# Attention in blocks of 64 tokens on 64x64 tiles of the array, with parts of the next product between its steps

## The chip, the core and the metric

The kernel runs on one core of a Trainium2 chip. The time is in device microseconds (us), and the kernel before has a median of 674.34 us over two runs (673.64 and 675.03). Engines: TensorE (PE, its weight loads apart as PEld), VectorE (DVE), ScalarE (ACT), GpSimd (POOL), and SyncE (SP), whose queue issues nearly all DMA transfers.

## The reference, cut to what matters

Inputs: q, k, v of shape (4, 8, 768, 64), fp32; one decay lam per head; then U (768, 32), V (32, 768), w_ch1 (512, 2048) and w_ch2 (2048, 512), which arrive as 64-bit numbers.

```
for b in range(12):                       # blocks of 64 tokens
    intra = (qb @ kb.T * Dmask) @ vb      # Dmask[i, j] = lam ** (i - j) for i >= j, else 0
    inter = (qb * lam ** (pos + 1)) @ kv_state
    out[block] = intra + inter
    kv_state = lam ** 64 * kv_state + (kb * lam ** (63 - pos)).T @ vb
x = out, as (4, 768, 512)                 # heads side by side
u = x + (x.T @ U @ V).T                   # mixing over the 768 tokens, rank 32
result = u + relu(u @ w_ch1) @ w_ch2
```

## The kernel before

The kernel has three stages.

**The front** walks through NS = 24 steps: 4 sequences of NT = 6 tiles of P = 128 tokens each, all 8 heads in a step (HP = 4 pairs of heads, two to the 128 rows of the array). Although the reference uses blocks of 64 tokens, a step treats its 128 tokens as one block, with a decay mask of 128 by 128 and one state update for the step. The work is cut into named pieces, and the list `pieces` is an order written out by hand: in this stage every engine runs its instructions in just this order. A step s has on PE: `prep` (transposes of q and k of step s + 1, L348, which ACT copies out as qt and kt, L351), `scores` (pss, L393), `inter` (q times the held state, px, L434), `intra` (masked scores times v, px, L446) and `state` (pkv, L411). DVE multiplies the scores by the mask (sm, L402) and adds up the state (kv, L419); POOL scales k (ks, L365) and the transposed q (qs, L376); ACT fades the old state (L385) and copies the result out (x_nat, L451). An fp32 matmul is two instructions in the profile.

Six to seven steps later a finished tile goes on: once a sequence has its six tiles, `low` (L461) makes x.T @ U, DVE and ACT split it into parts (`low_rows`, `next_of_low`), and `mix` (L506) multiplies by V; DVE adds that to x (L509). `turn` transposes u (L523), writes u to memory (u_d, issued on SP) and splits it into a high part, a low part and a difference (u_hl, u_d; L528, L539, L542, L543). Meanwhile `aside` converts the 64-bit weights into three such parts on DVE and ACT (L154 to L217); w1 tiles 0 and 1 are made in the front.

**The first product** takes w1 tile by tile (FT = 16) against u in NG = 6 groups of 512 tokens: `hidden` takes two groups at a time and makes for each 8 matmuls into pz (L722) and 4 into pd (L732). ACT takes pz out into a tile r (L728), DVE adds pd (L737), and SP writes r to memory. The first eight calls (`head`) also carry the last tiles' mix and turn, put between their matmuls by the lists `rest` and `at`.

**The second product** reads r back, applies the relu and splits it (L837 to L840), and multiplies with w2 (L855, L857, L859) into all eight PSUM banks, four pairs per group. `finish` takes each pair out through a tile o: ACT (L876), DVE (L880), POOL (L884), a write issued on SP (L885). The tiles r and o share one pool:

```
r_pool = ctx.enter_context(tc.tile_pool(name="r", bufs=4, reuse_waits="tile"))
...
o = r_pool.tile([P, C], FP32, tag="r", name="o")
```

From the end of `head` on, the order of instructions comes from the framework's planner and not from a list. A tile from a pool with n buffers waits until the tile n before it under the same tag has been read for the last time.

## Time and profile before

| | before |
|---|---|
| median of the runs | 674.34 us (673.64 to 675.03) |
| profiled execution, span from first to last instruction | 672.5 us |
| lowest and highest run less that span | 1.1 and 2.5 us |
| PE, PEld busy | 665.9 us (99%), 545.4 us (81%) |
| DVE, ACT, POOL busy | 496.6 (74%), 278.7 (41%), 112.8 us (17%) |
| front ends (first pz matmul starts) | 121.45 us |
| granted TensorE clock, mean | 0.999 of full |

The profiled execution has no time of its own beside its span; the runs lie 1.1 to 2.5 us above it. In the profile, a line like `28.78 1.16 PE L393 MATMUL ... x16` is a merged group: start and length in us, engine, line of the kernel, shape and count. A group's length includes the drain of its last matmul, so that the cost of a group in a stream of work is the distance from its start to the next group's start. PE counts as busy while any matmul is under way; that it is busy doesn't mean that it is at its peak.

### The profile page before, as it was taken

To read this page: it belongs to the slowest core of one execution; us is meant where nothing else is said; L and a number is where in the kernel's file an instruction comes from. 1 tells how busy PE (TensorE), PEld (TensorE's weight loads), DVE (VectorE), ACT (ScalarE), POOL (GpSimd) and SP (SyncE) were. 2 spreads that over 40 slices of the span, in tenths; PEclk is the share of its full clock that TensorE was granted. 3 is DMA by queue.
4 is the path that set the end of the run, shared out by engine and by line. 5 is a ranking of instruction groups with operands and counts; after the bars stand their busy time and mean duration, and the time that the engine had idled before them with its cause. 6 is when DMAs were issued, how large, how long until landed. Compare 5 with 4: busy or idle time off the path is not lost.

```text
span 672.5 us, 13170 instructions
## 1 busy us (share of the span) xinstructions
PE 665.9 (99%) x5124; PEld 545.4 (81%) x5124; DVE 496.6 (74%) x873; ACT 278.7 (41%) x517; POOL 112.8 (17%) x92
## 2 busy tenths in 40 slices
PE   9999999999999999999999999999999999999997
PEld 8888898787888888888888888888888888888885
DVE  4679999777999777777797255786586775865854
ACT  4675767454555444444455121332232322322320
POOL 4455667340000000000000000030030200300300
PEclk9999999999999999999999999999999999999999
DMA  9999993264776555555587999854363363443421
GB/s 208 214 228 239 237 232 109 84 215 156 235 276 240 204 203 204 204 203 204 203 280 253 325 314 387 291 185 140 94 206 107 110 204 94 158 155 95 161 89 62
DMA packets 131775, 131.27 MB, mean 195 GB/s; under 512 B 81346, under 2 KB 89794, under 8 KB 131714
## 3 DMA queue, kind: packets, MB, share of 16 engines
q1 hardware_dynamic: 130656, 130.18, 61.3%
q8 instruction: 40, 0.66, 0.4%
q10 hardware_dynamic: 1058, 0.26, 0.2%
q14 instruction: 21, 0.17, 0.1%
HBM read 80.09 MB, written 50.33 MB: 194 GB/s over the span
## 4 chain that ended last, share of the span: by engine, by line
PE 96%; DVE 2%; ACT 2%; issue 0%; DVEq 0%; ACTq 0%
PE pz L722 27%; PE pz L857 13%; PE pd L732 13%; PE pz L855 13%; PE pd L859 13%; PE pss L393 3%; PE px L446 3%; PE put L523 2%; PE pq L348 2%; PE px L434 1%; PE pkv L411 1%; PE pk L348 1%; PE pp L461 1%; PE pu L506 1%; PE idle L336 0%; ACT qt L351 0%
## 5 line engine op out<-in xcount | busy, mean ns | idle before, releaser
L722 PE MATMUL pz<-u_hl,w 128*128 128x512 f32 x768 | 190.4, 397 | 0.0
L722 PEld LDWEIGHTS pz<-u_hl,w 128*128 128x128 f32 x768 | 144.0, 188 | 35.5 <-issue 0.4
L857 PE MATMUL pz<-w_hl,m 128*128 128x512 f32 x384 | 151.1, 396 | 0.0
L855 PE MATMUL pz<-w_hl,m 128*128 128x512 f32 x384 | 150.9, 396 | 0.0
L859 PE MATMUL pd<-w_d,m 128*128 128x512 f32 x384 | 149.5, 396 | 0.0
L838 ACT ACTIVATE m<-mt 128x512 fp32r<-128x512 f32 x96 | 60.7, 633 | 196.0 <-PE pd L859 141.7
L839 DVE SCALAR_TENSOR_TENSOR m<-rm,m 128x512 fp32r<-128x512 f32 x96 | 71.4, 745 | 52.2 <-ACT m L838 52.1
L884 POOL TENSOR_TENSOR o<-o,u 128x512 f32<-128x512 f32 x20 | 29.9, 1529 | 447.3 <-DVE o L880 447.3
L737 DVE SCALAR_TENSOR_TENSOR r<-pd,r 128x512 f32<-128x512 f32 x96 | 61.8, 685 | 54.0 <-ACT r L728 43.5
L732 PE MATMUL pd<-u_d,w 128*128 128x512 f32 x384 | 98.6, 397 | 0.0
L728 ACT ACTIVATE r<-pz 128x512 f32<-128x512 f32 x96 | 52.2, 596 | 93.6 <-PE pz L722 92.9
L857 PEld LDWEIGHTS pz<-w_hl,m 128*128 128x128 f32 x384 | 72.3, 188 | 17.7
L855 PEld LDWEIGHTS pz<-w_hl,m 128*128 128x128 f32 x384 | 72.3, 188 | 17.6
L859 PEld LDWEIGHTS pd<-w_d,m 128*128 128x128 f32 x384 | 72.3, 188 | 17.6
L732 PEld LDWEIGHTS pd<-u_d,w 128*128 128x128 f32 x384 | 72.1, 188 | 17.3
L840 DVE SCALAR_TENSOR_TENSOR m<-m 128x512 fp32r<-128x512 f32 x96 | 69.0, 720 | 0.9
L837 DVE TENSOR_SCALAR mt<-rm 128x512 uint32<-128x512 uint32 x96 | 46.1, 481 | 28.0 <-DMA rm<-r_d 27.6
L402 DVE TENSOR_TENSOR sm<-pss,mask 128x512 f32<-128x512 f32 x48 | 30.8, 683 | 7.4 <-PE pss L393 7.3
L205 ACT CAST w<-wt 128x512 fp32r<-128x512 f32 x32 | 19.9, 622 | 30.5 <-DVE wt L202 23.4
L376 POOL TENSOR_TENSOR qs<-qt,powq 128x512 f32<-128x512 f32 x20 | 25.9, 1296 | 23.3 <-ACT qt L351 22.3
L446 PEld LDWEIGHTS px<-vraw,sm 128*64 128x64 f32 x768 | 24.7, 137 | 6.0 <-issue 2.4
L446 PE MATMUL px<-vraw,sm 128*64 128x64 f32 x768 | 28.3, 226 | 0.5 <-DVE sm L402 0.4
(88 smaller groups left out, 682.7 us busy)
## 6 DMA issues: line engine op xcount, KB each, us to landing
r_d<-r SPq DMA_DIRECT2D x96, 256.0 KB, 2.5
rm<-r_d SPq DMA_DIRECT2D x96, 256.0 KB, 2.7
words<-in_moe_w_ch_dram SPq DMA_DIRECT2D x30, 512.0 KB, 4.4
w_d<-w SPq DMA_DIRECT2D x16, 768.0 KB, 3.3
w_hl<-w_d SPq DMA_DIRECT2D x16, 512.0 KB, 6.2
vraw<-in_v_dram SPq DMA_DIRECT2D x24, 256.0 KB, 4.6
u_d<-x_nat SPq DMA_DIRECT2D x24, 256.0 KB, 3.5
u<-u_d SPq DMA_DIRECT2D x24, 256.0 KB, 4.1
```

Of the source, the lines that this page charges most:

```text
L446: nc.tensor.matmul(out=px[half[t], x, a, :], lhsT=sm[:, x, a, half[t]], rhs=vr[:, 2 * a + x, :], start=(first and a == 0), stop=(a == HP - 1),
L722: nc.tensor.matmul(out=acc[g][0], lhsT=w[:, n, ct, :], rhs=uhl[g][:, n, ct, :], start=(ct == 0 and n == 0), stop=(ct == CT - 1 and n == 1),)
L728: nc.scalar.mul(rs[g], acc[g][0], 4096.0 + 1.0)
L732: nc.tensor.matmul(out=acc[g][1], lhsT=w[:, 2, ct, :], rhs=ud[g][:, ct, :], start=(ct == 0), stop=(ct == CT - 1),)
L737: nc.vector.scalar_tensor_tensor(rs[g], acc[g][1], 4096.0, rs[g], ALU.mult, ALU.add)
L837: nc.vector.tensor_scalar(t.bitcast(U32), r.bitcast(U32), HI, None, ALU.bitwise_and)
L838: nc.scalar.activation(out=m[:, 0], in_=t, func=AF.Relu)
L839: nc.vector.scalar_tensor_tensor(m[:, 1], r, 0.0, hi, ALU.max, ALU.subtract)
L840: nc.vector.scalar_tensor_tensor(m[:, 2], hi, E, low, ALU.mult, ALU.subtract)
L855: nc.tensor.matmul(out=pz, lhsT=m[:, 0, cols], rhs=hl[:, 0], start=first, stop=False)
L857: nc.tensor.matmul(out=pz, lhsT=m[:, 1, cols], rhs=hl[:, 1], start=False, stop=end)
L859: nc.tensor.matmul(out=pd, lhsT=m[:, 2, cols], rhs=dd, start=first, stop=end)
```

## The change

Attention works in blocks of 64 tokens, two to a step. `scores` makes only the two diagonal 64 by 64 blocks of each head, `masked` is one DVE pass instead of two, `intra` multiplies each half with its own half of v. `state` makes a sum for each half block (two banks); the state between the halves, kvm, is a second DVE pass, and `inter` uses the held state for the first half and kvm for the second. Scores and px of a step share a tile sx of two banks, of which there are two. `state(s + 1)` comes before or after `intra(s)` in the step before its own; `masked` moves to the start of the next step, and `turn` comes one step later. ks, qs, qt and kt have one buffer instead of two, v's raw tile four instead of three.

A new piece `fill` makes half a unit of the first product (one w1 tile against 256 tokens) in the steps 10, 13 to 17 and 19 to 23, in the banks of mix and turn; `fill_end` adds pd and writes it out. w1 tiles 0 and 1 are converted earlier, and w1 tile 2 is made in the front, in a pool of its own. The first product's head is cut anew for what is left, partly with one group in a call. The tag tmp has two buffers instead of three, and the pool r three instead of four. The constants are made for 64 tokens, and the first ks and qs are made by DVE.

```diff
+    w1x_pool = mid_ctx.enter_context(tc.tile_pool(name="w1x", bufs=1, side="right"))
...
-        return wconv.tile([P, C], FP32, tag="tmp", bufs=3, name=name)
+        return wconv.tile([P, C], FP32, tag="tmp", bufs=2, name=name)
...
-            w1v[ft] = w1_pool.tile([P, 3, C], F32R, tag="w1", name="w1")
+            pool = w1x_pool if ft % 4 == 2 else w1_pool
+            w1v[ft] = pool.tile([P, 3, C], F32R, tag="w1", name="w1")
...
-            [P, H, D], FP32, tag=f"{name}raw", bufs=4 if name == "k" else 3, name=f"{name}raw"
+            [P, H, D], FP32, tag=f"{name}raw", bufs=3 if name == "q" else 4, name=f"{name}raw"
...
-            ts[s] = att.tile([P, HP, P], FP32, tag=name + "t", bufs=2, name=name + "t")
+            ts[s] = att.tile([P, HP, P], FP32, tag=name + "t", name=name + "t")
...
     def scale_k(s):
...
+        ks = att.tile([P, HP, 2, D], FP32, tag="ks", name="ks")
+        st.setdefault(s, {})["ks"] = ks
+        (nc.gpsimd if s else nc.vector).tensor_tensor(
+            out=ks,
+            in0=raw[s, "k"].rearrange("p (a x) d -> p a x d", x=2),
+            in1=rev.rearrange("p x a -> p a x").unsqueeze(3).broadcast_to([P, HP, 2, D]),
+            op=ALU.mult,
+        )
 
     def scale(s):
 
...
+        st[s]["qs"] = qs = att.tile([P, HP, P], FP32, tag="qs", name="qs")
+        i = slice(D if s % NT == 0 else 0, P)
+        (nc.gpsimd if s else nc.vector).tensor_tensor(
+            out=qs[:, :, i], in0=st[s]["qt"][:, :, i], in1=powq[:, :, i], op=ALU.mult
+        )
 
     def fade(s):
 
-        if 0 < s % NT < NT - 1:
-            st[s]["faded"] = faded = att.tile([P, HP, D], FP32, tag="faded", name="faded")
+        if s < NS and s % NT > 0:
+            faded[s] = att.tile([P, HP, D], FP32, tag="faded", name="faded")
             for a in range(HP):
-                nc.scalar.mul(faded[:, a, :], kv[s][:, a, :], lamc[:, a, :])
+                nc.scalar.mul(faded[s][:, a, :], kv[s][:, a, :], lamc[:, a, :])
 
     def scores(s):
         qt, kt = st[s]["qt"], st[s]["kt"]
...
+        st[s]["sx"] = sx = psf.tile([P, 2, N], FP32, tag="sx", bufs=2, name="sx")
+        st[s]["pss"] = pss = sx[:, :, 0 : HP * D].rearrange("p x (a i) -> p x a i", a=HP)
+        st[s]["px"] = sx[:, :, HP * D :].rearrange("p x (a e) -> p x a e", a=HP)
         for a in range(HP):
             for x in range(2):
                 for t in range(2):
                     nc.tensor.matmul(
-                        out=px[half[t], x, a, :], lhsT=st[s]["qs"][half[x], a, half[t]],
-                        rhs=kv[s][half[x], a, :], start=(a == 0), stop=False,
+                        out=pss[half[t], x, a, :], lhsT=kt[half[x], a, half[t]],
+                        rhs=qt[half[x], a, half[t]], start=True, stop=True,
+                    )
+
+    def masked(s):
+        st[s]["sm"] = sm = att.tile([P, 2, HP, D], FP32, tag="sm", bufs=1, name="sm")
+        nc.vector.tensor_tensor(
+            out=sm, in0=st[s]["pss"], in1=mask[:, :, :, 0:D], op=ALU.mult
+        )
+
+    def state(s, tags=("pq", "pk")):
+        c = s % NT
+        ks, vr = st[s]["ks"], raw[s, "v"]
+        ts = range(2 if c < NT - 1 else 1)
+        pkv = [one_bank([P, HP, D], "pkv", tags[t]) for t in ts]
+        for a in range(HP):
+            for x in range(2):
+                for t in ts:
+                    nc.tensor.matmul(
+                        out=pkv[t][half[x], a, :], lhsT=ks[half[t], a, x, :],
+                        rhs=vr[half[t], 2 * a + x, :], start=True, stop=True,
+                    )
+        st[s]["kvm"] = kvm = att.tile([P, HP, D], FP32, tag="kvm", name="kvm")
+        if c == 0:
+            nc.vector.tensor_copy(out=kvm, in_=pkv[0])
+        else:
+            nc.vector.tensor_tensor(out=kvm, in0=pkv[0], in1=faded.pop(s), op=ALU.add)
+        if c < NT - 1:
+            kv[s + 1] = att.tile([P, HP, D], FP32, tag="kv", bufs=2, name="kv")
+            nc.vector.tensor_tensor(out=kv[s + 1], in0=pkv[1], in1=kvm, op=ALU.add)
+
+    def inter(s):
+
+        px, qs = st[s]["px"], st[s]["qs"]
+        for a in range(HP):
+            for x in range(2):
+                for t in range(s % NT == 0, 2):
+                    held = st[s]["kvm"] if t else kv[s]
+                    nc.tensor.matmul(
+                        out=px[half[t], x, a, :], lhsT=qs[half[x], a, half[t]],
+                        rhs=held[half[x], a, :], start=(a == 0), stop=False,
                     )
 
     def intra(s):
         first = s % NT == 0
         sm, vr, px = st[s]["sm"], raw[s, "v"], st[s]["px"]
-        px = px[:, :, 0 : HP * D].rearrange("p x (a e) -> p x a e", a=HP)
-        for a in range(HP):
-            for x in range(2):
+        for x in range(2):
+            for a in range(HP):
                 for t in range(2):
                     nc.tensor.matmul(
-                        out=px[half[t], x, a, :], lhsT=sm[:, x, a, half[t]],
-                        rhs=vr[:, 2 * a + x, :], start=(first and a == 0), stop=(a == HP - 1),
+                        out=px[half[t], x, a, :], lhsT=sm[half[t], x, a, :],
+                        rhs=vr[half[t], 2 * a + x, :],
+                        start=(first and t == 0 and a == 0), stop=(a == HP - 1),
                     )
         xs[s] = x_pool.tile([P, C], FP32, tag="x", name="x_nat")
         nc.scalar.copy(xs[s].rearrange("p (a x e) -> p x a e", a=HP, x=2), px)
+        del st[s]
+        del raw[s, "v"]
+        load_next("v")
+
+    filled = []
+
+    def fill(ft, m, tags):
+
+        g, j = divmod(m, 2)
+        cols = slice(j * 2 * P, (j + 1) * 2 * P)
+        pz = one_bank([P, 2 * P], "pz", tags[0])
+        w = w1v[ft].rearrange("p n (c f) -> p n c f", f=P)
+        for ct in range(CT):
+            for n in range(2):
+                nc.tensor.matmul(
+                    out=pz, lhsT=w[:, n, ct, :], rhs=uhl[g][:, n, ct, cols],
+                    start=(ct == 0 and n == 0), stop=(ct == CT - 1 and n == 1),
+                )
+        r = att.tile([P, 2 * P], FP32, tag="rf", bufs=2, name="rf")
+        pd = one_bank([P, 2 * P], "pd", tags[1])
+        for ct in range(CT):
+            nc.tensor.matmul(
+                out=pd, lhsT=w[:, 2, ct, :], rhs=ud[g][:, ct, cols],
+                start=(ct == 0), stop=(ct == CT - 1),
+            )
+        nc.scalar.mul(r, pz, 4096.0 + 1.0)
+        filled.append((r, pd, r_d[ft][g][:, cols]))
+
+    def fill_end():
+        r, pd, to = filled.pop()
+        nc.vector.scalar_tensor_tensor(r, pd, 4096.0, r, ALU.mult, ALU.add)
+        nc.sync.dma_start(out=to, in_=r)
...
-    pieces = [("prep", 0), ("scale", 0), ("scores", 0), ("inter", 0), ("masked", 0)]
+    fills = {10: (0, 0)}
+    fills.update({13: (0, 1), 14: (1, 0), 15: (0, 2), 16: (1, 1), 17: (0, 3)})
+    fills.update({19: (1, 2), 20: (0, 4), 21: (1, 3), 22: (0, 5), 23: (1, 4)})
+
+    pieces = [("prep", 0, name, a0) for a0 in (0, 2) for name in "qk"]
+    pieces += [("scale", 0), ("scores", 0), ("prep", 1, "q"), ("prep", 1, "k")]
+    pieces += [("state", 0), ("inter", 0), ("masked", 0), ("scale_k", 1), ("fade", 1)]
     for s in range(NS):
         b, c = divmod(s, NT)
         done = s - NT - 1
         more = s + 1 < NS
-        step = [("prep", s + 1), ("scale", s + 1)] * more
+        turns = done > 0 and (done - 1) // TG < FG
+        rows = c == 0 and b > 0
+        step = [("scale_k", s + 1)] * (0 < s < NS - 1)
+        step += [("masked", s)] * (s > 0 and s not in fills)
         step += [("late", s - 1)] * (s == NT)
-        step += [("mix", done)] * (0 <= done < NS - NT - 1)
-        step += [("low", b - 1)] * (c == 0 and b > 0)
-        step += [("low_rows", b - 1)] * (c == 0 and b > 0)
-        step += [("intra", s)]
-        step += [("next_of_low", b - 1)] * (c == 0 and b > 0)
-        step += [("late", s)] * (s < NT - 1 or s == NT) + [("state", s)]
-        step += [("next_of_low", b - 1)] * (c == 0 and b > 0)
+        two = [("mix", done)] * (0 <= done < NS - NT - 1), [("turn", done - 1)] * turns
+        step += two[c == 1] + two[c != 1]
+        step += [("masked", s)] * (s in fills)
+        step += [("prep", s + 1, "q"), ("prep", s + 1, "k")] * (0 < s < NS - 1)
+        step += [("scale", s + 1)] * more
+        step += [("low", b - 1), ("low_rows", b - 1)] * rows
+        step += [("fill", *fills.get(s, ()), ("pt", "pu") if c == 1 else ("pu", "pt"))] * (s in fills)
+        early = s < NT or s in fills
+        main = [("intra", s)] + [("next_of_low", b - 1)] * rows
+        ahead_state = [("state", s + 1, ("pt", "pu") if s < NT else ("pq", "pk"))] * more
+        step += ahead_state + main if early else main + ahead_state
+        step += [("fill_end",)] * (s in fills)
+        step += [("late", s)] * (s < NT - 1 or s == NT)
+        step += [("next_of_low", b - 1)] * rows
         step += [("turned", done - 1)] * (done > 0) + [("late", s)] * (done >= 0)
-        step += [("next_of_low", b - 1)] * (c == 0 and b > 0)
-        step += [("scores", s + 1)] * more
-        step += [("aside", s)] * (s >= 2 * NT)
-        step += [("inter", s + 1), ("masked", s + 1), ("fade", s + 1)] * more
-        step += [("aside", s)] * (s < 2 * NT)
-        step += [("turn", done)] * (done >= 0 and done // TG < FG)
+        step += [("next_of_low", b - 1)] * rows
+        step += [("scores", s + 1), ("inter", s + 1), ("fade", s + 2)] * more
+        step += [("aside", s)]
         pieces += step
...
-        (w1_steps(0, True), (3, 4, 5, 6, 8, 9, 10, 11, 12, 13, 14)),
-        (w1_steps(1, True), (8, 9, 10, 11, 15, 16, 17, 18, 19, 20, 21)),
+        (w1_steps(0, True), (2, 2, 3, 4, 5, 6, 6, 7, 7, 8, 9)),
+        (w1_steps(1, True), (6, 7, 8, 9, 10, 10, 11, 11, 12, 12, 12)),
+        (w1_steps(2, True), (12, 13, 14, 15, 16, 17, 18, 19, 20, 21, 22)),
...
-    for name in "qkvkv":
+    for name in "vqkvqkv":
         load_next(name)
     aside(-1)
-    for name in "qkv":
+    for name in "kv":
...
-        r_pool = ctx.enter_context(tc.tile_pool(name="r", bufs=4, reuse_waits="tile"))
+        r_pool = ctx.enter_context(tc.tile_pool(name="r", bufs=3, reuse_waits="tile"))
...
-    turns = iter([0, 0, 0, 0] + [1, 0] * (NG * FT))
-
-    def hidden(ft, pair, before={}):
-
-        acc = dict(zip(pair, banks(len(pair), next(turns))))
-        count = iter(range(12 * len(pair)))
+    turns = iter([0] * 6 + [1, 0] * (NG * FT))
...
-    body = [(pair, ft) for ft in range(2, LAST) for pair in pairs]
+    body = [(pair, ft) for ft in range(3, LAST) for pair in pairs]
...
-        (0, 4, "turn", c0 - 2), (0, 6, "mix", c0 - 1), (0, 9, "low", b), (0, 14, "low_rows", b),
-        (0, 14, "next_of_low", b), (0, 14, "next_of_low", b), (0, 14, "next_of_low", b),
-        (0, 18, "turn", c0 - 1), (0, 22, "mix", c0),
+        (0, 8, "turn", c0 - 2), (0, 11, "mix", c0 - 1), (1, 3, "low", b), (1, 8, "low_rows", b),
+        (1, 8, "next_of_low", b), (1, 8, "next_of_low", b), (1, 8, "next_of_low", b),
+        (1, 12, "turn", c0 - 1), (1, 16, "mix", c0),
     ]
 
-    at = [(1, 5), (1, 17), (2, 4), (2, 17), (3, 3), (3, 10)]
+    at = [(1, 23), (2, 10), (2, 21), (3, 8), (4, 6), (5, 3)]
     for n, (unit, i) in enumerate(at):
         if n + 1 < NT:
             rest.append((unit, i - 3, "mix", c0 + n + 1))
         rest.append((unit, i, "turn", c0 + n))
     run["enter"] = enter_first_product
-    head = [(pair, ft) for two in (pairs[:2], pairs[2:]) for ft in (0, 1) for pair in two]
-    side = list(zip((0, 3, 3, 3, 4, 4, 4, 4), w1_steps(2)))
-    for i, (pair, ft) in enumerate(head):
+    head = [([(2, slice(2 * P, N))], 1), (pairs[0], 2), (pairs[1], 2), ([3], 0), ([3], 1)]
+    head += [([g], ft) for g in pairs[2] for ft in range(3)]
+    side = list(zip((3, 5, 6, 6, 7, 8, 9, 10), w1_steps(3)))
+    for i, (groups, ft) in enumerate(head):
...
-    for ft in range(3, FT - 1):
-        side += w1_steps(ft) + w2_steps(ft - 3)
-    side += w2_steps(FT - 4)
+    for ft in range(4, FT - 1):
+        side += w1_steps(ft) + w2_steps(ft - 4)
+    side += w2_steps(FT - 5) + w2_steps(FT - 4)
```

## The prediction

> **What bounds the kernel now.** I read the page first, then the chain of waits, then the engines by stretch of the front, then single steps in order of time.
>
> ```profile
> span 672.5 us, 13170 instructions
> ...
> PE 96%; DVE 2%; ACT 2%; issue 0%; DVEq 0%; ACTq 0%
> ```
>
> TensorE is the bound from end to end: the chain that ends last is 96% PE. A change pays only by PE time taken away, or by PE idle time filled. The front (24 attention steps) ends at 121.45 us, where the first pz matmul starts. These are its four batches of six steps, with the columns PE, PEld, DVE, ACT, POOL busy, clock, DMA share and GB/s:
>
> ```profile
> 6.40:32.60 26.20, 26.15 (x577) 23.43 (x576) 14.58 (x33) 15.86 (x39) 14.00 (x12) 1.00 0.96 220
> 32.60:62.50 29.90, 29.27 (x649) 26.08 (x645) 24.40 (x40) 20.38 (x48) 17.43 (x15) 1.00 0.99 239
> 62.50:92.50 30.00, 29.54 (x756) 26.54 (x750) 28.92 (x52) 20.70 (x46) 20.86 (x16) 1.00 0.94 232
> 92.50:121.40 28.90, 28.51 (x746) 25.71 (x742) 26.42 (x48) 18.38 (x42) 18.33 (x14) 1.00 0.51 137
> ```
>
> PE is full, but two others stand close behind it: the DMA engines in the first three batches (0.94 to 0.99) and DVE in the third (28.92 of 30.00). Whatever PE saves there meets them next. One early and one late step, each group's cost being its start to the next start:
>
> ```profile
> 27.23 1.15 PE L446 MATMUL px<-vraw,sm 128*64 128x64 f32 x32
> 28.21 0.64 PE L411 MATMUL pkv<-vraw,ks 128*64 128x64 f32 x16
> 28.78 1.16 PE L393 MATMUL pss<-qt,kt 64*128 64x128 f32 x16
> 29.87 0.69 PE L434 MATMUL px<-kv,qs 64*64 64x64 f32 x32
> 30.50 0.66 PE L348 MATMUL pq<-ident,qraw 128*128 128x128 f32 x4
> ...
> 108.50 1.10 PE L393 MATMUL pss<-qt,kt 64*64 64x128 f32 x32
> 109.43 0.64 PE L434 MATMUL px<-kv,qs 64*64 64x64 f32 x32
> 110.00 0.66 PE L523 MATMUL put<-ident,x_nat 128*128 128x128 f32 x4
> ...
> 111.69 1.15 PE L446 MATMUL px<-vraw,sm 128*64 128x64 f32 x32
> 112.67 0.64 PE L411 MATMUL pkv<-vraw,ks 128*64 128x64 f32 x16
> 113.24 1.10 PE L393 MATMUL pss<-qt,kt 64*64 64x128 f32 x32
> ```
>
> Early: intra 0.98, state 0.57, scores 1.09, inter 0.63 us. Late: 0.98, 0.57, 0.93, 0.57. A late step is 113.24 - 108.50 = 4.74 us.
>
> **Part 1, attention on 64x64 tiles.** Before, over 24 steps: intra 24 x 0.98 = 23.5; state, in 20 steps, 11.4; scores 12 x 1.09 + 12 x 0.93 = 24.2; inter 10 x 0.63 + 10 x 0.57 = 12.0; together 71.1 us. After, scores keep the four tiles of the late row with half the moving columns: half of 0.93, and I take 0.44. That agrees with the inter row, which has just this shape: 32 instructions in 0.57, of which I put 0.13 down to the change to the 128-row shape that follows. State now has this shape too (each half block its own sum), so 0.44 with 32 instructions, 0.22 in the last step of a sequence, where before there was none; inter 0.44, and 0.22 in the first step. Intra uses only the two tiles on the diagonal, as many as its 128*64 row keeps busy now, so it stays: 0.95. Sum: scores 10.6, state 9.7, inter 9.7, intra 22.8, and 24 x 0.2 for one change of shape into and out of the run of four groups, 4.8: 57.6 us. **Part 1 is -13.5 us on PE**, all of it on the path as long as PE stays the bound.
>
> [...] The row has 32 in 0.57 us with the change of shape, 18 ns each, so I go by the row.
>
> **Part 2, eleven half units.** A pair of units now takes 24 matmuls from one pair's start to the next:
>
> ```profile
> 156.93 3.75 PE pz L722 x16
> ...
> 162.55 3.74 PE pz L722 x16
> ```
>
> That is 5.62 us, 234 ns a matmul. Half a unit leaves the later product with 12 x 0.117 = 1.40, eleven of them with 15.4 us. In the front each is 12 matmuls of 256 columns, which the trace has nowhere. Its floor is the weight load: two back to back take 0.30 us and one 0.19, so 0.11 apart; its ceiling is a load not hidden at all, 0.19:
>
> ```profile
> 123.00 0.30 PEld L722 LDWEIGHTS pz<-u_hl,w 128*128 128x128 f32 x2
> ```
>
> 11 x 12 x 0.11 = 14.5; x 0.19 = 25.1 us. Loads do run under the previous matmul here, so I take 0.13, a little over half of 234: 17.2 us, that is **+1.8 net** (bounds -0.9 and +9.7). Moving gains nothing by itself while PE is full; it gains where PE would have stood idle. With each fill go 0.3 us on ACT (half of L728's 596 ns), 0.42 on DVE (as kv L419 at 256 columns) and a write issued on SP (about 0.35). They hide under PE: a fill step is 4.74 - 0.6 + 1.56 = 5.7 us of PE against about 4.7 of DVE.
>
> **Part 3, DVE and POOL.** Per step the mask falls from two to one 0.68 us pass, and kvm adds 0.42: -0.26. The third w1 tile adds its chain of 0.42 + 0.42 + 0.69 + 0.70 + 0.69 + 0.44 + 0.68 + 0.73 = 4.8 us of DVE to the third and fourth batch and takes it out of the head; its four loads of 128 KB go onto SP among the raw loads. POOL has L365 24 times instead of 20 at 1.06 and L376 at about 1.3: some 3.8 a step with L543. All that costs nothing while a step takes over 4.7 us of PE; without that cover each us of it counts. The turn of a tile, with its u_d write on SP, comes one step later, behind the mask in DVE's queue; state comes a step earlier and takes pq and pk after ACT's copies of qt and kt (2 x 0.59), under intra or a fill. qt, kt, qs and ks have one buffer instead of two: the next qt copy waits for POOL's qs pass and the last scores, both done a group earlier. I cost these at nothing too; the cover is the 1.7 us of put, pq, pk and mix between them, and if it is gone a step waits up to POOL's 1.3. In the head, units of one group halve the time between two evictions to 2.8 us; ACT's 0.60 and DVE's 0.69 for each fit in.
>
> **Part 4, waits that come.** (a) Start: the DMA engines give 220 / 0.96 = 229 GB/s, so a 256 KB tile is 1.14 us and a step's three 3.4. PE's early step falls from 4.29 to about 3.5, and one more v tile and two w1 loads stand ahead of q and k of step 7. Of the 4 us that PE would save up to there, and with scale_k(0) and scale(0) now on DVE ahead of the first mask, I expect 3 us as waiting. (b) Each low product feeds mix one step later through DVE 1.2, DVE 1.25 and ACT 0.62 with the kv passes between: about 5.7 us from low's start, as now (65.65 to 71.43). PE's own work between is down to 4.1, so 1.5 us of stall at steps 13 and 19 and 2 at step 7: 5 us. (c) At step 13 the last three w1(1) passes (1.9 us) stand in DVE's queue ahead of ut and x_nat; the fill's pz needs the bank that they drain: 1.3 us. Together 9.3. The same kind of waiting in the front of before (waits of PE and PEld with a named releaser, overlaps taken off) is about 5.5. **Net +3.8** (bounds -3 and +9).
>
> **Part 5, three r buffers.** The pool also holds the four o tiles of finish. The fourth must now wait until the first has been written out:
>
> ```profile
> 441.50 2.59 ACT L876 ACTIVATE o<-pz 128x512 f32<-128x512 f32 x4
> ...
> 443.00 5.99 POOL L884 TENSOR_TENSOR o<-o,u 128x512 f32<-128x512 f32 x4 [291.31 <-DVE o L880]
> 444.35 1.59 SPq L885 DMA_DIRECT2D out_dram<-o  x2
> 445.64 0.40 PE L855 MATMUL pz<-w_hl,m 128*128 128x512 f32 x1
> ```
>
> The first out write is issued at 444.35 and lands about 2 us later, 446.4. Then ACT's fourth pass 0.6 to 447.0 and DVE's 0.68 to 447.7. PE wants that pz bank at 445.64 and its pd bank 0.47 later: a stall of up to 1.9, at five group ends 9.5 us. The lower bound is 0: this part isn't ordered by hand (L840 and L839 stand in the trace in changing order), and the planner can hand PE the next step's products while bank three is held. I take 0.4 each, nearer to the lower end: **+2.0**. In the first product the third buffer is free in time: the r writes land in 2.5 us, and a unit pair takes 5.62.
>
> **Sum.** -13.5 + 1.8 + 3.8 + 2.0 = -5.9: span 672.5 to 666.6. The runs' median, 674.34, lies 1.8 above the profiled span, so **668.4 us**.
>
> **Rivals.**
> 1. *The fills find idle PE and nothing else waits* (0.20): the half matmul at 0.11 (-0.9), group ends free (0), front waits as now (0): 672.5 - 13.5 - 0.9 = 658.1, with 1.8 about 660; with 2 us fewer waits 658. For it: DVE and DMA have room once steps grow to 5.7. Against: (b) above has no cover in steps 7, 13 and 19, which hold the low products or follow them.
> 2. *The o wait in full, or the half matmul bound by its load* (0.22): +7.5, or about +7.9, gives 676, no change. For it: the 4.9 us from ACT to landing is plain in the rows.
> 3. *Slower: intra's two tiles take turns* (0.08). Both row halves write one PSUM bank (px of one x); no row of before has that, since its row halves x write different banks. If they alternate, its pace goes from 29 to 58 ns: 32 x 29 ns x 24 = 22 us, 690. From 37 ns on the gain of the sum is gone (768 x 7.7 ns = 5.9), from 54 on the kernel is 2% slower. Against it: the halves write different partitions. [...]
>
> **How the numbers follow.** My forecast has 0.50: a gain of about 1%. The range 656 to 680 holds it, nearly all of rival 1 and rival 2; rival 3 is left out. A measurement of this kernel tells about 2% from no change, that is below 660.9 or above 687.8. Faster by over 2% needs most of rival 1 (0.13) and a tail of the forecast (0.04): 0.17. Slower by over 2% is rival 3 with a part of its weight gone to milder forms: 0.06. Within: 0.77.
>
> **What would show it.** Scores, state and inter at about 0.44 us each, intra at 0.95; twelve 256-wide matmuls in 1.56; the first whole unit of the later product at about 130 us, 8 to 10 later than 121.45, with 5.5 fewer units behind it; gaps of 1 to 2 us ahead of mix L506 after each low; at 441-like places a gap in PE ahead of the fourth o. I am wrong if intra's pace is near 58 ns, if the front ends before 124 (waits smaller), or after 135 (DVE the bound).

## The result, and the profile after

The changed kernel takes 720.83 us (median of 2 runs, 718.91 to 722.75) against 674.34 before: a ratio of 1.069, with a 95% interval from 1.062 to 1.076. The forecast was 668.4 with a range of 656 to 680; the time lies 52 us above the one and 41 above the other. The profiled execution has a span of 717.1 us where the sum gave 666.6.

First the span, the chain of work that ended last, the row of the granted clock in 40 slices, and the row of TensorE's instruction queue, from the page of the changed kernel:

```profile
span 717.1 us, 14723 instructions
...
PEclk9989989999999999999999999999999999999999
...
q8 instruction: 46, 0.75, 0.4%
...
PE 84%; DVE 8%; issue 3%; DMA 2%; ACT 2%; SPq 0%; POOL 0%; DVEq 0%; ACTq 0%; POOLq 0%
```

PE had 96% of the chain and has 84%. What is new is mainly DVE 8% (2% before), "issue" 3% (PE stood still and nothing in the profile held it) and DMA 2%. The clock falls in two of the first six slices. Now the front in four batches of six steps (the last ends with the front; the number behind the stretch is its length, then PE, PEld, DVE, ACT, POOL busy, clock, DMA share, GB/s):

```profile
6.40:42.50 36.10, 29.82 (x836) 26.35 (x838) 21.11 (x46) 16.94 (x44) 16.45 (x15) 0.96 0.99 202
42.50:81.20 38.70, 33.08 (x913) 29.41 (x906) 25.94 (x45) 24.98 (x59) 18.21 (x16) 0.95 0.82 188
81.20:131.30 50.10, 39.26 (x927) 36.09 (x926) 33.85 (x58) 22.91 (x56) 20.60 (x19) 0.90 0.60 150
131.30:168.00 36.70, 33.07 (x829) 29.61 (x827) 26.02 (x52) 20.44 (x50) 18.84 (x16) 1.00 0.36 103
```

The front ends at 167.99 us, where the first pz L783 starts, instead of 121.45. Apart from the DMA engines in the first batch (0.99) nothing is full: in the third batch PE works 39.3 of 50.1 us, DVE 33.9, and the share of the DMA engines is 0.60. So the engines are not short of throughput there; they wait. What PE does when it isn't held up is as foreseen. This is one late step with a fill, from mix to mix (start, duration of the group, then the group):

```profile
124.40 0.50 PE L551 MATMUL pu<-vp 128*128 128x512 f32 x1
...
125.96 1.19 PE L479 MATMUL pz<-u_hl,w 128*128 128x256 f32 x8
...
127.74 0.69 PE L427 MATMUL pkv<-vraw,ks 64*64 64x64 f32 x32
128.26 1.03 PE L458 MATMUL sx<-vraw,sm 64*64 64x64 f32 x29
...
130.23 0.50 PE L551 MATMUL pu<-vp 128*128 128x512 f32 x1
```

From 124.40 to 130.23 are 5.83 us (5.7 was the estimate). State takes 0.52 from start to start, the fill 1.78; in the lines left out intra takes 0.83, scores, from 129.08, 0.5, and inter, from 129.59, 0.6 with the change of shape behind it. The loss is therefore between the groups. The longest waits of PE in the front (line, what it waited for, us in total, times, longest):

```profile
PE pz L479 <- DVE u_hl L584: 5.0, 2, 3.9
...
PE sx L447 <- issue: 3.6, 4, 1.7
...
PE pu L551 <- ACT vp L541: 3.5, 3, 1.3
...
PE sx L458 <- DVE sm L415: 2.9, 1, 2.9
...
PE pu L551 <- ACT faded L398: 2.0, 1, 2.0
```

Three kinds: waits for a DVE pass (u_hl, sm, and x_nat with 3.6 us at the low product), waits for the end of the low chain (vp), and waits for nothing ("issue": 3.6 us at inter, another 2.4 at scores L408 and 0.9 at pk). The 2.0 us at mix that the last line puts down to ACT are very probably of the third kind too; experiments 3 and 5 say why. The trace's record of the granted clock adds a fourth cost: full clock comes at 19.1 us (8.9 before; at 15.07, 29 matmuls of intra still take 1.86 us, at 128.26 they take 1.03; the 0.96 of the first batch's row leaves out the time before 19.1), and the clock is at half again from 39.6 to 46.4, 94.2 to 101.0 and 111.2 to 114.7, each time in or just after a gap of 2 to 4 us.

The second product takes 286.7 us (from 430.48 to the end) against 273.9. This is the first of its five group ends:

```profile
478.81 0.60 ACT L946 ACTIVATE o<-pz 128x512 f32<-128x512 f32 x1 [2.08 <-DMA out_dram<-o]
...
481.95 0.50 PE L929 MATMUL pd<-w_d,m 128*128 128x512 f32 x1 [1.52 <-DVE o L950]
```

ACT waits 2.08 us until an o tile has been written out; its pass for the fourth o comes late, DVE's behind it (at 481.22), and PE stops ahead of pd, after a shorter stop at pz (0.16 at 479.46). What is left of the first product behind the front came as foreseen: 262.5 us (277.1 before), and 277.1 less eleven half units of 1.40 is 261.7.

### The profile page after: what moved, and what is told of

Its sections match the earlier page's. It is cut to its first block, busy times and chain, and to the rows that moved or that the text cites. A ratio compares the mean times of both kernels' runs of the same rounds, so it can differ in the third digit from the quotient of the medians.

```text
span 717.1 us, 14723 instructions
## 1 busy us (share of the span) xinstructions
PE 676.8 (94%) x5836; PEld 552.8 (77%) x5836; DVE 499.7 (70%) x887; ACT 285.4 (40%) x539; POOL 116.5 (16%) x98
## 4 chain that ended last, share of the span: by engine, by line
PE 84%; DVE 8%; issue 3%; DMA 2%; ACT 2%; SPq 0%; POOL 0%; DVEq 0%; ACTq 0%; POOLq 0%
PE pz L783 22%; PE pd L929 12%; PE pz L927 11%; PE pz L925 11%; PE pd L797 11%; PE sx L458 3%; PE pkv L427 2%; PE sx L447 2%; PE pz L479 2%; PE pq L367 1%; PE pk L367 1%; PE sx L408 1%; DVE m L909 1%; PE put L568 1%; PE pu L551 1%
## 5 line engine op out<-in xcount | busy, mean ns | idle before, releaser
L783 PE MATMUL pz<-u_hl,w 128*128 128x512 f32 (+1 forms) x728 | 179.8, 396 | 0.3 <-ACT r L793 0.3
L783 PEld LDWEIGHTS pz<-u_hl,w 128*128 128x128 f32 x728 | 136.1, 188 | 33.4 <-ACT r L793 0.7
L925 PE MATMUL pz<-w_hl,m 128*128 128x512 f32 x384 | 153.4, 399 | 0.7 <-ACT o L946 0.3
L927 PE MATMUL pz<-w_hl,m 128*128 128x512 f32 x384 | 152.9, 398 | 0.0
L797 PE MATMUL pd<-u_d,w 128*128 128x512 f32 (+1 forms) x364 | 94.0, 396 | 0.0
L804 DVE SCALAR_TENSOR_TENSOR r<-pd,r 128x512 f32<-128x512 f32 (+1 forms) x91 | 58.8, 682 | 42.5 <-ACT r L793 21.5
L793 ACT ACTIVATE r<-pz 128x512 f32<-128x512 f32 (+1 forms) x91 | 50.4, 591 | 76.4 <-PE pz L783 72.8
L389 POOL TENSOR_TENSOR qs<-qt,powq 128x512 f32<-128x512 f32 (+1 forms) x23 | 28.0, 1218 | 29.3 <-ACT qt L370 28.7
L458 PE MATMUL sx<-vraw,sm 64*64 64x64 f32 x768 | 29.4, 228 | 2.9 <-DVE sm L415 2.9
L458 PEld LDWEIGHTS sx<-vraw,sm 64*64 64x64 f32 x768 | 26.5, 142 | 5.8 <-DVE sm L415 3.4
L464 ACT COPY x_nat<-sx 128x512 f32<-128x512 f32 x24 | 14.1, 586 | 39.0 <-PE sx L458 36.8
```

Source lines behind the costliest of these rows:

```text
L458: nc.tensor.matmul(out=px[half[t], x, a, :], lhsT=sm[half[t], x, a, :], rhs=vr[half[t], 2 * a + x, :], start=(first and t == 0 and a == 0) ...
L783: nc.tensor.matmul(out=acc[g, cols][0][:, 0 : cols.stop - cols.start], lhsT=w[:, n, ct, :], rhs=uhl[g][:, n, ct, cols], start=(ct == 0 and ...
L793: nc.scalar.mul(rs[one], acc[one][0][:, 0 : rs[one].shape[1]], 4096.0 + 1.0)
L797: nc.tensor.matmul(out=acc[g, cols][1][:, 0 : cols.stop - cols.start], lhsT=w[:, 2, ct, :], rhs=ud[g][:, ct, cols], start=(ct == 0), stop= ...
L804: nc.vector.scalar_tensor_tensor(rs[one], acc[one][1][:, 0 : rs[one].shape[1]], 4096.0, rs[one], ALU.mult, ALU.add)
L925: nc.tensor.matmul(out=pz, lhsT=m[:, 0, cols], rhs=hl[:, 0], start=first, stop=False)
```

## The experiments

Two theories stood against each other for the front. **Q**: the order of DVE's queue. Passes that nobody hurries for (the conversion of w1, three tiles instead of two by step 22) stand ahead of sm, x_nat and u_hl, and PE waits for these. **F**: PE runs out of instructions. Each matmul here comes with a weight load of its own; the q8 row has 46 packets for 5836 matmuls and 5836 loads, so a packet is some 254 instructions or 127 matmuls. If a packet can't be there in time, PE stops in the middle of a group. That is what this part of the timeline looks like, inside the 32 matmuls of one scores group, whose inputs all had been there at its start:

```profile
24.86 0.63 PE L408 MATMUL sx<-qt,kt 64*64 64x64 f32 x27
26.46 0.27 PE L408 MATMUL sx<-qt,kt 64*64 64x64 f32 x2 [0.97 <-issue]
```

A third theory, **P**, was the prediction's own: PE's work counts and little else. Experiments 1 to 8, 10 and 12 are one run each, and front ends are read from one profile each. The front end moved by 2.5 us between two kernels with the same front (168.0 and, in experiment 1, 165.5), so smaller differences of it aren't read, and the larger ones are good to about that much.

**1. A fourth o buffer.**

```diff
-        o = r_pool.tile([P, C], FP32, tag="r", name="o")
+        o = (r_pool if n < 3 else m_pool).tile(
+            [P, C], FP32, tag="r" if n < 3 else "o4", bufs=3 if n < 3 else 1, name="o"
+        )
```

> The changed kernel with a fourth buffer for the o tiles of the second product (the fourth o of a group comes from another pool). If the gaps of PE at the five group ends (1.9 us each ahead of pd L929, with 0.3 to 0.6 us stretched matmuls around them) are the wait for the third buffer, the second product goes from 286.7 us back to 274 to 275 us and the span from 717 to about 705; the front does not move. Rival: PE waits there for POOL's or DVE's slower passes and not for a buffer; then the gaps stay and the span is 716 to 718.

Measured: 703.42 us, span 701.6. The row of the second product in it:

```profile
427.37:701.60 274.23, 270.38 (x1153) 216.62 (x1151) 190.57 (x316) 70.70 (x115) 29.86 (x20) 1.00 0.47 154
```

274.2 us: the second product is back at its old time, and PE has no wait with a releaser left in it. The third buffer costs 286.7 - 274.2 = 12.5 us, 2.5 at each end. The other 3 us of this run are nearly all the front's scatter.

**2. The change without its half units.** No half units in the front; the head as before, with the third w1 tile. The new order of passes and the conversion of the third w1 tile in the front stay.

```diff
-    fills = {10: (0, 0)}
-    fills.update({13: (0, 1), 14: (1, 0), 15: (0, 2), 16: (1, 1), 17: (0, 3)})
-    fills.update({19: (1, 2), 20: (0, 4), 21: (1, 3), 22: (0, 5), 23: (1, 4)})
+    fills = {}
...
+    head = [(pair, ft) for two in (pairs[:2], pairs[2:]) for ft in (0, 1) for pair in two]
+    head += [(pair, 2) for pair in pairs]
```

> The attention on 64x64 tiles alone: no half units in the front, all units of the first product behind it as in the kernel before (w1 of unit row 2 still made in the front). Three theories for the front, which ended at 121.45 us before the change and at 168 with it. (P) Only PE's own work counts: 24 steps of some 3.9 us and 15 us of start and low chains, end at about 109. (Q) DVE's queue: the same DVE passes stand ahead of what PE waits for, 3.8 and 4.2 us at steps 12 and 13 and 3 us at step 4, nothing in between: end at about 118 to 122. (F) PE runs out of instructions: a block of 128 matmuls with their weight loads can't start earlier than about 4.4 us after the one before while the DMA engines are full; a step has 141 matmuls, so 4.5 to 5 us a step: end at 125 to 132, with gaps of 1 to 2 us that have no releaser (issue) every 128 matmuls.

Measured: 715.42 us, front end at 146.8. That is later than all three theories said, and 25 us later than with the old attention, although PE's attention groups take less time. So most of the loss comes without the fills, from the new attention and what was moved with it (this run doesn't part the two): with the fills the front is another 21.2 us longer, of which they are 19.6 themselves, for 15.4 us that they take from the later product. PE's waits in this front hold both kinds side by side: 8.1 us for sm and 4.3 for x_nat on DVE, 3.4 us at scores and 1.8 at inter without a releaser.

Neither theory is enough by itself. The long waits on DVE are at the steps that Q named; in between are stops without a releaser.

**3. No conversion of the second and third w1 tile.**

```diff
-        (w1_steps(1, True), (6, 7, 8, 9, 10, 10, 11, 11, 12, 12, 12)),
-        (w1_steps(2, True), (12, 13, 14, 15, 16, 17, 18, 19, 20, 21, 22)),
+        (w1_steps(1, True)[:4], (6, 7, 8, 9)),
+        (w1_steps(2, True)[:4], (12, 13, 14, 15)),
```

> The changed kernel without the conversion passes of the second and third w1 tile in the front (their loads stay; the first tile stands in for them, so the result is another). (Q) If these passes in DVE's queue make PE wait, the gaps ahead of pp L506 (3.8 us) and of the fill pz L479 (4.2 us) at steps 12 and 13 and the drop of the clock behind them go: the front ends at 155 to 158 instead of 168. (F) The gaps without a releaser, some 11 us in all, stay as they are; the rest of the gain is then still missing, the end stays far above 130.

Measured: 712.95 us, front end at 160.7, somewhat later than expected. The two gaps at steps 12 and 13 (3.6 and 3.9 us in the profile) are gone, so these are DVE's passes, as Q says. The waits without a releaser stay, as F says, and even grow from 6.9 to 10.8 us (4.9 at inter, 3.5 at scores, 2.3 at mix): where PE no longer waits for DVE, it runs into more of these stops, so what the two causes cost can't simply be added. The clock still falls to half, now from 74.6 to 81.4, beginning in a stop of 2.8 us without a releaser, and from 105.3 to 108.7, behind the one of 2.3 us at mix. That one stands at the same matmul as the 2.0 us which the changed kernel's profile put down to ACT, so ACT's pass was not what it waited for there. This is why the two gaps are so long, in DVE's queue of the changed kernel around step 12, with one line each of POOL (its ks pass, at 81.18, is the other) and of PE:

```profile
81.26 1.53 DVE L180 SCALAR_TENSOR_TENSOR sc<-words,sc 128x512 uint32<-128x512 uint32 x1 [1.07 <-ACT sc L162]
82.82 1.72 DVE L185 SCALAR_TENSOR_TENSOR wf<-m,sc 128x512 f32<-128x512 f32 x1
...
85.06 0.68 DVE L554 TENSOR_TENSOR x_nat<-pu,x_nat 128x512 f32<-128x512 f32 x1
```

```profile
82.73 1.26 POOL L389 TENSOR_TENSOR qs<-qt,powq 128x512 f32<-128x512 f32 x1 [0.49 <-ACT qt L370]
```

```profile
85.79 1.52 PE L506 MATMUL pp<-x_nat,u_w 128*32 128x128 f32 x48 [3.57 <-DVE x_nat L554]
```

Two conversion passes of 1.53 and 1.72 us (0.68 each where POOL rests, at 51.61 and 144.11 us) stand ahead of sm and x_nat. The low product was moved by the change to the bank pu, which x_nat drains, so it now waits for that pass; before, it wrote the bank pq, which ACT drains.

**4. Without 63 of the 72 q, k and v loads.**

```diff
     def load(name, s, engine):
         b, c = divmod(s, NT)
+        if s >= 3:
+            raw[s, name] = kept[name, s % 3]
+            return
```

> The changed kernel with the q, k and v tiles of the first three steps used again in all later steps, so 63 of the 72 loads of 256 KB are left out. (F) If instructions come late because their packets share the DMA engines with these loads, the gaps without a releaser shrink from 1 to 2 us to under 0.5 and the front ends 8 to 11 us earlier, near 158. If their way is long even on idle engines, the gaps stay at 1 to 2 us. (Q) The long stalls on DVE's passes stay; only the waits for a raw tile (under 1 us in all) go: end at 166 to 168.

Measured: 712.29 us, front end at 160.1, so 7.9 us earlier, as F said for instructions that share the DMA engines. But PE's named "issue" waits went only from 6.9 us (3.6, 2.4 and 0.9) to 3.0, although the DMA share is 0.15 to 0.17 from 40 us on: four such stops, the longest 1.0 us, are left with nearly idle engines.

**5. The small matmuls by themselves.** This measures the disputed cost without any wait between engines.

```python
    small(40)   # per group 16 calls: 64x64 weights, 64 columns, four tiles
    wide(16)    # the same with 128 columns
    for t in raws[-3:]:                       # wait for the last of 72 loads
        warm(1, t.rearrange("p h d -> p (h d)")[:, 0:P])
    warm(60, one[:, 1, :])
    small(41)
    wide(17)
```

> Not the computation, but its matmuls alone, without waits, output zeros. First, while 72 loads of 256 KB run, 40 groups of 32 matmuls of 64x64 with 64 columns (the shape of state), then 16 groups of 32 of 64x64 with 128 columns (twice as long each); then, with the loads done, 41 and 17 such groups again. (P) If only TensorE's work counts, the small ones run at 13 to 16 ns a matmul throughout, the wide ones at about 29, with and without loads. (F) If instructions come in blocks of 128 matmuls that can't follow each other faster than some 4.4 us under load, the small ones take 34 ns each on average, with a gap of about 2 us after every 128, and the wide ones about 34 too, with short gaps; without loads the gaps are shorter or gone.

TensorE's timeline, small ones under loads, wide ones under loads, small ones without, wide ones without:

```profile
16.07 2.09 PE L95 MATMUL small<-two,one 64*64 64x64 f32 x128 [1.52 <-issue]
20.07 2.09 PE L95 MATMUL small<-two,one 64*64 64x64 f32 x128 [1.91 <-issue]
...
55.10 3.72 PE L107 MATMUL wide<-two,one 64*64 64x128 f32 x128 [2.25 <-issue]
```

```profile
112.85 2.09 PE L95 MATMUL small<-two,one 64*64 64x64 f32 x128 [2.18 <-issue]
116.58 2.10 PE L95 MATMUL small<-two,one 64*64 64x64 f32 x128 [1.63 <-issue]
...
141.86 10.95 PE L107 MATMUL wide<-two,one 64*64 64x128 f32 x384 [0.75 <-issue]
```

This settles that F exists. The stops come after exactly 128 matmuls, that is after 128 weight loads and 128 matmuls, again and again, with nothing to wait for. Inside a block the small ones run at 14.8 ns at full clock (128 in 2.09 us, the last one's end included); with the stops 1280 of them take 40.0 us, 31.3 ns each, under loads, and still 27.4 from 112.85 on, where the DMA engines are idle (share 0.02). A block can follow the one before after 4.0 to 4.8 us under loads and 3.5 to 4.0 without. The wide ones need 3.72 us a block: without loads they run almost through (30.5 ns each), under loads they still stop. Under loads the clock fell to half twice, each time about 1 us after the end of a stop of 2.7 us (0.83 on average over the small ones).

The DMA records of the traces tie the stops to the instructions themselves. Each packet of TensorE's instruction queue is 16 KB (q8: 29 packets and 0.48 MB here, 46 and 0.75 in the changed kernel), and every stop without a releaser over 0.3 us, 22 here and 52 in the kernels of experiments 1 to 11 and the changed one, ended 1.3 to 1.7 us after such a packet had ended: here packets end at 18.66 and 23.51 us, and blocks start at 20.07 and 24.89. In the changed kernel a packet ends at 109.28, and the mix that was said to wait for ACT starts at 110.82, 1.5 us later. The time from block to block is made of three parts: from the start of a block to the start of the next packet 1.0 to 1.3 us on idle engines and 1.3 to 2.5 under loads, the packet itself 0.9 to 1.9, and then the 1.3 to 1.7.

**6. The kernel before, with its early scores in 32 matmuls instead of 16.**

```diff
-                for rows in half if s >= 2 * NT else [slice(0, P)]:
+                for rows in half:
```

> The kernel before with the scores of the first twelve steps cut into four tiles as in the later steps: 32 matmuls of half the height instead of 16. (P) By the rows of the scores (1.09 us in 16 matmuls, 0.93 in 32) PE saves 12 x 0.16 = 1.9 us: the front ends at about 119.6 instead of 121.45. (F) A step then has 125 to 133 matmuls in 4.1 us where a block of 128 needs about 4.4: gaps without a releaser take the gain away, and the front ends at 121.5 to 124.

Measured: 673.39 us against 674.07, front end at 120.6: 0.85 of the 1.9 us, a difference too small to be read. One stop of 0.74 us without a releaser appears, up to 98.97 us, in a late step that the edit leaves as it was. An early step carries 120 matmuls in 4.07 us here (104 in 4.29 before) without a stop, with longer matmuls among the short ones. This run doesn't tell the theories apart.

**7. Idle matmuls in step 0.**

```diff
-    pieces += [("scale", 0), ("scores", 0), ("prep", 1, "q"), ("prep", 1, "k")]
-    pieces += [("state", 0), ("inter", 0), ("masked", 0), ("scale_k", 1), ("fade", 1)]
+    pieces += [("scale", 0), ("scores", 0), ("busy", 3, "pt"), ("prep", 1, "q")]
+    pieces += [("busy", 3, "pt"), ("prep", 1, "k"), ("busy", 3, "pt"), ("state", 0)]
+    pieces += [("busy", 4, "pt"), ("inter", 0), ("busy", 3, "pt"), ("masked", 0)]
+    pieces += [("scale_k", 1), ("fade", 1)]
```

> The changed kernel with 16 idle matmuls of 128x128 put between the pieces of step 0, where PE waits for tiles and copies. If the slow start is a clock that comes to full late (at 19.1 us; 8.9 before the change) because PE kept stopping, the clock is full at 11 or before and intra of step 1 starts at about 16 instead of 20.4: 4 us off the front and the span. Rival: the waits themselves set the pace there, and the idle matmuls only stand in the way: 0 to +1 us.

Measured: 714.18 us, full clock from 8.3 us, front end at 162.3, which is 5.7 us earlier. In the changed kernel PE stops at the start for 0.56 us on a raw q tile, 0.33 on the copy kt and 0.52 on the new state of step 0; the idle matmuls fill these stops, and the clock is full 11 us earlier. But the 5.7 us are not the start's: intra of step 1 starts at 18.6 instead of 20.4, not at the expected 16, and intra of step 14 at 106.6 instead of 106.8. The waits in between have taken the gain back. 3.5 of the 5.7 us come from step 14 to step 15 alone (5.8 us instead of 9.3), where the changed kernel has its 2.0 us stop at mix with the half clock behind it and this run, whose blocks of 128 matmuls end elsewhere, has none. So the slow start by itself is worth 1.8 us at step 1, and its share of the front end isn't shown.

**8. Half as many matmuls, twice as wide.** The counter-test to 5 in the kernel itself: scores, state, inter and intra each in half as many calls.

```diff
-        for a in range(HP):
+        for a in (0, 2):
...
-                        out=pss[half[t], x, a, :], lhsT=kt[half[x], a, half[t]],
-                        rhs=qt[half[x], a, half[t]], start=True, stop=True,
+                        out=pss[half[t], x, a : a + 2, :], lhsT=kt[half[x], a, half[t]],
+                        rhs=qt[half[x], a, :], start=True, stop=True,
```

> The changed kernel with scores, state, inter and intra in half as many matmuls of twice the columns (128 for 64, two heads' columns with one head's weights, so the result is another): TensorE has the same work, but a step's four groups are 64 matmuls and not 128. (F) If blocks of 128 matmuls that arrive too late are a cause, the gaps without a releaser (some 11 us in the front) go, and the front ends at 155 to 159 instead of 168. (Q) If all waiting comes from DVE's queue, nothing changes: 166 to 169. If the wide ones cost more than twice the narrow ones, the groups show it: state above 0.52 us, scores above 0.47.

Measured: 705.40 us, front end at 155.5, 12.5 us earlier (10.0 against experiment 1, which has the same front). Among PE's waits no "issue" is left, and the 2.0 us at mix are gone as well; those on DVE are in sum what they were (sm 4.4 us, u_hl 3.7, x_nat 3.4, against 2.9, 5.0 and 3.6).

A step like the one above (5.83 us) takes 5.69 here, so by an estimate from this one step 24 x 0.14 = 3.4 of the 12.5 us are a little less work, and some 9 are the blocks.

**9. Mended: o buffer, start, passes spread over the steps.** Experiments 1 and 7, and:

```diff
-        (v_steps(), (0, 0, 3, 3, 4, 4, 4, 5, 4, 5)),
-        (w1_steps(0, True), (2, 2, 3, 4, 5, 6, 6, 7, 7, 8, 9)),
-        (w1_steps(1, True), (6, 7, 8, 9, 10, 10, 11, 11, 12, 12, 12)),
-        (w1_steps(2, True), (12, 13, 14, 15, 16, 17, 18, 19, 20, 21, 22)),
+        (v_steps(), (0, 0, 3, 3, 4, 4, 5, 5, 6, 5)),
+        (w1_steps(0, True), (2, 2, 3, 4, 6, 7, 7, 8, 8, 9, 9)),
+        (w1_steps(1, True), (6, 7, 8, 9, 10, 10, 11, 11, 12, 13, 13)),
+        (w1_steps(2, True), (12, 13, 14, 15, 16, 17, 17, 19, 20, 21, 22)),
```

> The changed kernel with three mends that leave the result as it is: the fourth o buffer, the idle matmuls of step 0, and DVE's conversion passes at no more than two a step, none beside the low chains but one. Adding up: 15.5 us from the buffer, 5.7 from the start, 5 to 9 from the passes (w1's without any were worth 7.3, the V passes hold PE up for 3 us at step 4): 687 to 691 us, front end at 152 to 157. (F) The gaps every 128 matmuls stay, so it does not come under the kernel before (674).

Measured: 700.66 us (median of 4; ratio to the kernel before 1.040, 1.037 to 1.042), front end at 162.9, no earlier than in experiment 7. Of the 15.5 us put down to the buffer 3 had been the front's scatter, and the spreading brought nothing to the end. Step 4 lost its wait in part (1.6 us instead of 2.9), but step 11 still had its two passes ahead of the low product (3.5 us, 3.6 before), and the passes that I moved to steps 9 and 17 made new waits of 1.8 and 2.7 us there. At intra of step 14 the run was 6.0 us ahead of experiment 7; it lost 3.6 of them by step 15, with a stop of 2.0 us without a releaser and half clock, and 4.0 at the new wait behind step 17, again with half clock. Moving passes from step to step moved the waits along with them.

**10. The same with half as many matmuls.**

> The mended kernel with the four attention groups in half as many matmuls of twice the columns (another result). (F) The gaps every 128 matmuls go as well: 8 to 12 us less than the mended kernel, front end at 142 to 146, 676 to 682 us. Only the predicted low chains (4 us), one step of DVE and the clock are then left above the 130 us that were predicted. (Q) Same as the mended kernel.

Measured: 692.19 us, front end at 154.3: 8.6 us less than experiment 9, again without "issue" waits. The expected total was missed by 10 us, as much as experiment 9 missed its own.

**11. The passes moved within the step.** Experiment 9's o buffer and start; the conversion passes now come after mask, x_nat, ut and u_hl of a step and ahead of kvm.

```diff
+        step += [("aside", s)]
         step += ahead_state + main if early else main + ahead_state
...
-        step += [("aside", s)]
         pieces += step
```

(Which step has which pass is as in experiment 9, but for three: two of V's passes change places between steps 5 and 6, and the third pass of the third w1 tile is back at step 18.)

> The mended kernel again, but with the conversion passes of a step moved in DVE's queue from the end of the step, ahead of the next step's mask, x_nat, ut and u_hl, to behind these four. (Q) The waits of PE for sm, x_nat and u_hl that the mended kernel still has in the front (some 13 us: 1.8, 1.7, 2.0, 3.8, 0.7, 2.9) go, and some 2 us come for kvm, which now stands behind the passes: the front ends at 152 to 155 instead of 162.9, the run is at 690 to 694. If it is DVE's load and not its order, the waits only change their names, and the time stays at 699 to 702.

Measured: 695.18 us (median of 4; ratio 1.031, 1.027 to 1.036), 5.5 us less than experiment 9. In the profiled runs (693.27 against 701.04) the front ends at 155.0, 7.9 us earlier. PE's longest waits there:

```profile
PE sx L447 <- DVE kvm L435: 4.2, 4, 2.5
PE sx L447 <- issue: 4.1, 4, 2.0
```

The waits for sm, u_hl and the low product's x_nat are gone, and kvm has come in their place, with 5.4 us in all (L435 and L433) instead of the 2 expected. The stops without a releaser have grown from 4.2 to 8.6 us (3.1 of them at intra, 1.4 at scores), as in experiment 3. DVE's load is the same and the plan by steps nearly so; it was the order: Q holds in this form.

**12. The same with half as many matmuls.**

> The same with the four attention groups in half as many matmuls of twice the columns (another result). (F) Another 8 to 10 us off the front, which ends at 143 to 146; 680 to 684 us. What is then left above the predicted 130 us is the low chains, the start and single copies. (Q) alone: the same as with all the matmuls.

Measured: 685.68 us, front end at 146.8, 8.2 us less. No "issue" waits are left; kvm has 6.4 us, vp 3.4, v's raw tile 1.1.

No mended version came under the kernel before; experiment 11 is 3% above it.

## Why the prediction was wrong

By its own steps, in the order of the sum:

- **What bounds the kernel.** Right for the kernel before. The step "a change pays only by PE time taken away" was carried over to a kernel with other, shorter work on PE, and that is where it fails: the chain went from 96% to 84% PE.
- **Part 1, attention: right as work, wrong as time.** The groups came out as priced: scores 0.5 (0.44), state 0.52 and inter 0.6 with their changes of shape, intra 0.83 (0.95). Experiment 2 shows that without the fills the front is 25 us longer, not 13.5 less 3.8 shorter. Besides the order in part 3, the missing term is the number of instructions: an early step went from 104 matmuls to 136 and was to take 3.5 us, and experiment 5 shows that 128 short matmuls with their loads take at least 4.0 to 4.8 us while the DMA engines are full. The prediction had the counts (x577 to x756 matmuls a batch in its rows) and, in the page of before, 40 instruction packets of 0.66 MB in all, and never set one against the other. Before, 125 matmuls in 4.74 us stayed under that pace. Halving the number of matmuls took 12.5, 8.6 and 8.2 us off the front (experiments 8, 10 and 12), of which by estimate 3.4 are less work in their groups: **5 to 9 us**.
- **Part 2, fills.** 1.78 us instead of 1.56, of which 0.21 is the change to the 64x64 shape behind it; eleven times 0.22 is 2.4 us. Within the bounds. The half units came out of the later product as foreseen (262.5 us against 261.7).
- **Part 3, DVE and POOL at nothing: wrong.** The cover named for it was "a step takes over 4.7 us of PE" against DVE's load. The load did fit: DVE was never full. What counts is the place in DVE's queue: one conversion pass of 0.7 us that takes 1.4 to 1.7 beside POOL's passes (L211 1.43, L185 1.72), ahead of a pass that PE waits for, is a gap. Moving the passes behind those (experiment 9 against 11) gave 7.9 us of front in the profiled runs and 5.5 in the medians; leaving out two tiles' conversion gave 7.3. The step "the fill's pz needs the bank that they drain: 1.3 us" was right in place and came to 3.9: beside POOL's passes the three conversion passes took 4.3 us (1.25, 1.43 and 1.63), not 1.9. That low's product had been moved to the bank pu, which x_nat drains on DVE, was not seen at all: 3.6 us. The trace shows which passes are stretched: L185 takes 1.72 us beside POOL's passes and 0.68 at 144.11 us, where they leave it alone, while sm's pass (L415) takes 0.68 to 0.69 beside them as without them. The kernel before shows it too: L210 takes 0.68 us in the median, and 1.30 and 1.29 in the two passes that ran beside POOL's, at 74.58 and 109.03 us.
- **Part 4, waits that come: mis-sized.** The low chains cost waits of 1.3, 1.1 and 1.1 us at steps 7, 13 and 19, against 2, 1.5 and 1.5: right in place, a little less in size. The start was expected to cost 3 us as waiting for loads; PE waited 0.6 us for a raw tile, and what the late clock cost there was gone again by step 14 (experiment 7). Nothing in the sum stood for the clock, though three of the gaps of 2 to 4 us were paid a second time by matmuls at half speed behind them: from 39.6 us on PE is busy for 13.3 us of the front at half clock, about 6.6 us lost by estimate.
- **Part 5, three r buffers: wrong choice between the ends.** The upper end was 1.9 us a group end (its own rows make it 447.7 less 446.1, that is 1.6), and 0.4 was taken because the planner might order around it. It came to 12.5 in all against 2.0: at each of the five ends the full wait, 1.7 at pd and 0.3 at pz from one matmul's start to the next less the usual 0.23, and behind the last one 3.4 us at half clock.

Added up against the profiled span: the sum has the front end at 129 (121.45 - 13.5 + 17.2 + 3.8), it was 168.0: 39.0. The group ends add 12.5 - 2.0 = 10.5, the later product 0.8. That is 50.3 of the 50.5 us. Of the front's 39.0, the order of the passes (experiment 9 against 11) takes 7.9 and the number of matmuls (11 against 12) 8.2; experiment 7 ended 5.7 earlier, of which no part is shown to be the start's. 17.8 are left in experiment 12 (146.8 against 129), among them 2.4 for the fills, 6.4 of waits for kvm, 1.1 for a raw tile and, by estimate, 4.6 for 9.2 us of busy PE at half clock. The rest stays open, and since the causes hide behind one another, no share is exact.

**The rivals.** The second was right in its first half, the o wait in full, and its time (676) was far too low because it left the other terms as they were. The third, the only one on the slow side, is refuted: intra's 32 matmuls take 0.83 us with both row halves in one bank, 26 ns each, not 58. The slow case that came, PE short of instructions and DVE's queue in the wrong order, was not among the rivals, so 0.06 for slower stood on the wrong mechanism. Of the marks named, "after 135: DVE the bound" was also wrong as it was put: the front ended at 168 with DVE busy for 107 of 162 us.

## What to carry to other kernels

Splitting matmuls into smaller tiles can save TensorE's work and still add to its instructions (here 104 matmuls in an early step became 136): divide the number of matmuls and weight loads of a stretch by 256 and compare with the 4.0 to 4.8 us a block that experiment 5 measured with full DMA engines (3.5 to 4.0 with idle ones) before counting the gain. Moving one wait away can uncover the next, so test the causes together as well as one by one. An engine with room in its load still holds up another if passes that nobody waits for stand in its queue ahead of passes that somebody waits for, so price a moved pass by what is queued behind it. Where a buffer is taken away and the trace shows the whole way of its next use, take the full wait, and leave room for the clock that a gap can take with it (here 3.4 us at half clock behind the one of 2.0 us at mix).

## What the runs showed of the hardware that was not expected

- In experiment 5 TensorE stopped after every 256 instructions (128 weight loads, 128 matmuls) when these were short: 3.5 to 4.0 us from block to block with idle DMA engines (share 0.02), 4.0 to 4.8 with full ones (0.96). Leaving out most loads in the kernel (experiment 4) more than halved the stops (6.9 to 3.0 us) but did not end them. Each stop over 0.3 us ended 1.3 to 1.7 us after a 16 KB packet of TensorE's instruction queue; the profile can also put such a stop down to an engine that was done (2.0 us at mix).
- Within a block of experiment 5, matmuls of 64x64 weights and 64 columns on four tiles started every 14.8 ns on average.
- In the changed kernel three gaps of 2.0, 2.9 and 3.9 us in the front came with 3.4 or 6.8 us at half the TensorE clock; another of 3.6 us (from 82.2 us) did not. Of five gaps of 1.5 us at the group ends only the last was followed by half clock, for 3.4 us.
